# DFT over 3136 points factored 56 by 56 instead of 64 by 49, step 1 in products of 256 columns, and six forms of the block of step 2 and residual

## The chip, the cores and the metric

The kernel runs on one core of one Trainium2 chip (trn2). The metric is the device time of one execution in microseconds (us); lower is better.

## The reference

What must be computed, cut to what matters (batch 8, sequence 3136, width 256; 4*256 = 1024 hidden):

```
def _attn_ref(x):
    X = np.fft.fft(x, axis=1)          # over 3136 positions
    X = np.fft.fft(X, axis=2)          # over 256 channels
    return X.real.astype(np.float32)

def _moe_ref(x, g_ln, w_ch1, w_ch2):
    mu, var = mean and variance of x over the channels
    xn = (x - mu) / np.sqrt(var + 1e-06) * g_ln
    ch = np.maximum(xn @ w_ch1, 0.0) @ w_ch2
    return (x + ch).astype(np.float32)
```

The input of the second function is the output of the first.

## The kernel before

The transform over 3136 positions is split as 64 times 49. **Step 1** (`step1`, L247) multiplies by the 64-point table, for two positions of the 49 at a time (both parities stacked on 128 partitions). The positions are paired by symmetry, so there are 14 slots of pairs, taken two at a time in 7 units per batch. For batch 0 the products are in full f32 (L255, L257); for batches 1 to 7 each operand is split in a rounded f32r part and its rest, and the unit is three f32r products of 512 columns with stationary tables of 128 by 128 (L262: `fl` with `t1_hi`, `fh` with `t1_lo`, `fh` with `t1_hi`). The folds that make the operands are `fold_zw` and `fold_eo` (L207 to L214) and `fold_lo` (L225), on POOL from batch 1 on. The result is copied to `s1` by ACT (L265), stored to DRAM (`store1`, L269), and read back with positions on partitions (`relayout`, L276). `ends` and `step1_ends` (L184, L233) do the same for two leftover channels with small f32 products (L237, L238, L241).

**Step 2** (`step2`, L299) multiplies by the twiddled 49-point tables in full f32: 16 groups of two units per batch, 98 columns each (99 and an extra product with 50 columns, L313, for the group that holds frequency 0), two products a group. One call does two groups, so there are 8 calls a batch and 64 in all. Each f32 product appears in the trace as two weight loads and two matmul instructions. ACT and DVE take the result from PSUM into the chunk `ck` and its f32r parts `ckh`, `ckl` (L330 to L334).

The rest works on **chunks** of 256 frequencies (49 of them, the last one 264 wide), in **slots** `s = 8c + f` for chunk `c` and hidden block `f`. In each slot `moe1_a` (L354) does 6 f32r products of 256 columns and `moe2` (L404) does 12, the latter for the hidden block three slots earlier; between them ACT and DVE make the hidden values (L359 to L369). `residual` (L422, products at L428) does the channel transform of the chunk in full f32 with 129 and 130 columns, for two halves `i` of the chunk; it gives the residual and the norm's statistics. `finish` (L473) joins both.

The order of each engine is written out by hand. The main loop runs over the slots; what else is done in a slot stands in two lists, `late` (before `moe2`) and `after` (behind it). `step2` for chunk `c + 1` and `residual` for chunk `c` are both put behind slot `8c + 5`, in that order; this run of f32 products is called the **block** below. `steps1` places the 7 units of step 1 of a batch at slots counted back from the slot `need`, at which the batch is first used; `behind` shifts a unit by two slots where a block has two calls of `step2`. Most units stand at the slot of a block and so directly behind it, since `joined` is added last. PSUM has one bank with the tag `y`, which serves step 1 from batch 1 on, the ends, and every second `step2` of a block with two.

Before the loop, the start loads `x` of batch 0 and the weights, runs step 1 of batch 0 on PE as the units arrive, stores, reads back, and converts the weights (given as 64-bit words) on DVE and ACT.

The loop of slots reads:

```
for s in range(6, last):
    moe1_b(s - 1)
    moe1_a(s)
    for fn, args in late.get(s, ()):
        fn(*args)
    moe2(s - lag)
    for fn, args in after.get(s, ()):
        fn(*args)
```

Of the kernel before, what the change touches and what calls it, by code (L numbers as in the profile page):

```python
# [51 lines left out]
def runs():

    units = [unit for g in range(16) for unit in (g, 16 + g)]
    return [r for unit in units for r in (((49, unit),) if unit else ((24, 64), (24, 32)))]


def group_bounds():
    return [0] + [99 + 98 * g for g in range(16)]


def tables():
    u = np.arange(64)[:, None]
    t1 = np.zeros((64, 64))
    t1[:, :33] = np.cos(2 * np.pi * u * np.arange(33) / 64)
    t1[:, 33:] = np.sin(2 * np.pi * u * np.arange(1, 32) / 64)
    th = np.zeros((64, 64))
    th[:, 1:32] = -np.sin(2 * np.pi * u * np.arange(1, 32) / 64)
    th[:, 33:] = np.cos(2 * np.pi * u * np.arange(1, 32) / 64)
    tu = np.zeros((128, 388))  # L70
    for par in range(2):
        s = slice(64 * par, 64 * par + 64)
        tu[s, s] = t1
        tu[s, 128 + 64 * par:192 + 64 * par] = -t1
        tu[s, 256 + 64 * par:320 + 64 * par] = th
        tu[s, 384 + 2 * par] = 1.0
        tu[s, 385 + 2 * par] = np.cos(np.pi * np.arange(64))
    vs = ((0, np.arange(1, 15)), (1, np.append(np.arange(15, NV), 0)))
# [68 lines left out]
def tile_kernel(ctx: ExitStack, tc: tile.TileContext, x, g_ln, w1, w2, tu, tab, tz, ty, tw, out):  # L147
# [710 lines left out]
```

## Time and profile before

| | |
|---|---|
| median of 2 runs | 1009.55 us (1008.93 to 1010.18) |
| span of the profiled execution | 1008.9 us |
| granted clock of TensorE, mean | 1.000 of full speed |
| busy: PE / PE weight loads / DVE / ACT / POOL | 99% / 97% / 81% / 53% / 25% |
| matmul instructions | 8289 |

The profiled execution agrees with the lower of the two runs. "PE" is the matmul row, "PEld" the weight loads beside it. The ends of matmuls are modelled, so successive matmuls overlap in the listing and a busy share says little; the distance from one start to the next is what PE really spends on one. A group of rows in the profile gives the mean of the listed durations, in ns.

### The profile page before, as it was taken

What the parts mean: (1) busy time and instruction counts of PE and PEld (TensorE: products, weight loads), DVE (VectorE), ACT (ScalarE), POOL (GpSimd) and SP (SyncE); (2) the same over time, 40 slices, a digit from 0 to 9 for tenths busy, and PEclk for the clock granted to TensorE, in tenths of its full rate; (3) what the DMA queues carried; (4) which work ended last, traced back from release to release, by engine and by line L of the source; (5) the groups of instructions that cost most, each with busy time, mean ns of one, the idle gap of its engine ahead of it and who ended that gap; (6) DMA issues with size and microseconds to landing.
All of it is one profiled execution on the core that took longest, in us unless ns stands there. A gap on an engine that the chain in (4) does not pass through costs nothing.

```text
span 1008.9 us, 21765 instructions
## 1 busy us (share of the span) xinstructions
PE 998.4 (99%) x8289; PEld 976.5 (97%) x8289; DVE 817.2 (81%) x2190; ACT 534.7 (53%) x1416; POOL 248.5 (25%) x278
## 2 busy tenths in 40 slices
PE   9899999999999999999999999999999999999998
PEld 6699999999999999999999999999999999999998
DVE  6688887888778788878887888888788878887887
ACT  3555555555555555555555555554555554554553
POOL 1146533134213232312341224123323200000000
PEclk9999999999999999999999999999999999999999
DMA  9943352214221261121521242211311112100101
GB/s 343 265 164 95 116 168 74 85 53 136 85 93 55 74 177 65 56 85 60 158 84 54 84 130 91 94 54 63 116 43 43 54 55 83 41 24 22 43 22 43
DMA packets 41528, 92.10 MB, mean 91 GB/s; under 512 B 4176, under 2 KB 18704, under 8 KB 40528
## 3 DMA queue, kind: packets, MB, share of 16 engines
q1 hardware_dynamic: 40016, 88.87, 26.8%
q8 instruction: 66, 1.08, 0.5%
q0 software_dynamic: 320, 1.05, 0.3%
q10 hardware_dynamic: 1088, 0.79, 0.2%
q14 instruction: 38, 0.31, 0.1%
HBM read 50.32 MB, written 40.37 MB: 90 GB/s over the span
## 4 chain that ended last, share of the span: by engine, by line
PE 93%; DVE 4%; ACT 2%; DMA 1%; issue 0%; SPq 0%; DVEq 0%; ACTq 0%
PE acc L404 51%; PE ab L354 26%; PE ps L309 6%; PE psy L428 4%; PE ps L262 3%; DVE h_lo L369 1%; PE pw L682 1%; PE ps L255 1%; DMA scratch<-s 1%; PE ps L257 1%; DVE h L360 1%; DVE h L361 1%; ACT h_hi L368 0%; DMA s<-scratch 0%; ACT asb L359 0%
## 5 line engine op out<-in xcount | busy, mean ns | idle before, releaser
L404 PE MATMUL acc<-w_hi,h_lo 128*128 128x256 f32 x1568 | 437.9, 279 | 0.2 <-DVE h_lo L369 0.2
L404 PE MATMUL acc<-w_lo,h_hi 128*128 128x256 f32 x1568 | 437.7, 279 | 0.0
L404 PE MATMUL acc<-w_hi,h_hi 128*128 128x256 f32 x1568 | 437.6, 279 | 0.0
L368 ACT ACTIVATE h_hi<-h 128x512 fp32r<-128x512 f32 x392 | 249.3, 636 | 308.4 <-DVE h L361 308.3
L369 DVE SCALAR_TENSOR_TENSOR h_lo<-h,h_hi 128x512 fp32r<-128x512 f32 x392 | 282.0, 719 | 158.1 <-ACT h_hi L368 157.0
L404 PEld LDWEIGHTS acc<-w_hi,h_lo 128*128 128x128 f32 x1568 | 296.7, 189 | 0.6 <-DVE h_lo L369 0.4
L404 PEld LDWEIGHTS acc<-w_lo,h_hi 128*128 128x128 f32 x1568 | 295.4, 188 | 0.0
L404 PEld LDWEIGHTS acc<-w_hi,h_hi 128*128 128x128 f32 x1568 | 295.1, 188 | 0.0
L354 PE MATMUL ab<-ckl,w_hi 128*128 128x256 f32 x768 | 218.5, 285 | 1.8 <-DVE h L361 1.8
L354 PE MATMUL ab<-ckh,w_lo 128*128 128x256 f32 x768 | 214.9, 280 | 0.5 <-ACT ckh L330 0.3
L354 PE MATMUL ab<-ckh,w_hi 128*128 128x256 f32 x768 | 214.5, 279 | 0.0
L225 POOL TENSOR_TENSOR fl<-f,fh 128x512 fp32r<-128x512 f32 x49 | 64.2, 1309 | 518.6 <-ACT fh L219 512.4
L360 DVE TENSOR_TENSOR h<-asb,ab 128x256 f32<-128x256 f32 x384 | 158.2, 412 | 1.5 <-ACT asb L359 1.5
L361 DVE TENSOR_TENSOR h<-asb,ab 128x256 f32<-128x256 f32 x384 | 158.1, 412 | 0.0
L354 PEld LDWEIGHTS ab<-ckl,w_hi 128*128 128x128 f32 x768 | 145.3, 189 | 5.9 <-ACT w_hi L539 1.5
L354 PEld LDWEIGHTS ab<-ckh,w_lo 128*128 128x128 f32 x768 | 144.7, 188 | 3.1 <-ACT ckh L330 0.5
L354 PEld LDWEIGHTS ab<-ckh,w_hi 128*128 128x128 f32 x768 | 144.6, 188 | 0.0
L359 ACT COPY asb<-ab 128x256 f32<-128x256 f32 x384 | 137.8, 359 | 8.1 <-PE ab L354 6.2
L265 ACT COPY s<-ps 128x508 f32<-128x508 f32 x56 | 32.7, 584 | 64.9 <-PE ps L262 51.0
L309 PE MATMUL ps<-tab_s,s 112*128 112x98 f32 (+1 forms) x512 | 65.6, 273 | 1.5 <-DMA s<-scratch 1.5
L309 PEld LDWEIGHTS ps<-tab_s,s 112*128 112x128 f32 x512 | 61.9, 192 | 2.0 <-issue 2.0
L330 ACT CAST ckh<-ps 128x392 fp32r<-128x392 f32 (+49 forms) x112 | 39.7, 356 | 40.6 <-PE ps L309 40.4
(108 smaller groups left out, 980.5 us busy)
## 6 DMA issues: line engine op xcount, KB each, us to landing
xs<-x SPq DMA_DIRECT2D x56, 512.0 KB, 3.8
out<-o SPq DMA_DIRECT2D x96, 256.0 KB, 2.0
scratch<-s SPq DMA_DIRECT2D x49, 256.0 KB, 2.3
s<-scratch SPq DMA_DIRECT2D x7, 1792.0 KB, 9.8
w1p_all<-w SPq DMA_DIRECT2D x8, 512.0 KB, 8.3
scratch<-s POOLq DMA_DIRECT2D x4, 256.0 KB, 6.3
s<-scratch SPq DMA_DIRECT2D x2, 448.0 KB, 5.3
s<-scratch SPq DMA_DIRECT2D x1, 896.0 KB, 11.2
```

What stands on the lines that cost most here:

```text
L225: nc.gpsimd.tensor_tensor(out=lo, in0=f, in1=hi.bitcast(F32), op=ALU.subtract)
L265: nc.scalar.copy(s[:, :, :, :127], ps[:, :, :, :127])
L309: nc.tensor.matmul(ps[:, h, k0 - base:k1 - base], s2[b][:KP, g, 128 * h:128 * h + 128], tab_s[:, h, k0:k1], start=(h == 0 and g == 2 * j), ...
L330: nc.scalar.copy(hi, src)
L354: nc.tensor.matmul(pt, wt[wi][:, j, fs], ch[xi][:, j, :w], start=(n == 0), stop=(n == 2))
L359: nc.scalar.copy(asb[:, :w], pa)
L360: nc.vector.tensor_tensor(out=h[:, :w], in0=asb[:, :w], in1=pb, op=ALU.add)
L361: nc.vector.tensor_tensor(out=h[:, w:], in0=asb[:, :m], in1=pb[:, :m], op=ALU.subtract)
L368: nc.scalar.activation(h_hi, h, AF.Relu)
L369: nc.vector.scalar_tensor_tensor(out=h_lo, in0=h, scalar=0.0, in1=h_hi.bitcast(F32), op0=ALU.max, op1=ALU.subtract)
L404: nc.tensor.matmul(acc[c, i][:, side], hs[xi][:, h0:h0 + 128], ws[wi][:, f], start=(f == 0 and side == 0 and n == 0), stop=(f == 7 and n = ...
L428: nc.tensor.matmul(ps[:, j, :129 + j], ck[:, j], ty_s[:, j, :129 + j], start=(j == 0), stop=True, skip_group_check=True)
```

## The change

The DFT is factored 56 by 56. A unit has 56 frequencies; there are 14 groups a batch, 112 columns each, 7 calls of `step2` a batch and 56 in all. The slots of pairs are now 15: 7 units of two slots, and an eighth unit (index `NU`) of one slot, which holds the positions that are multiples of 56 and has its own input `x0` and its own tile `xz`. Step 1 works on 112 partitions with tables of 112 by 112. From batch 1 on, step 1 does its three passes for each slot by itself, in products of 256 columns: six products for a unit of two slots, three for the eighth. Units of step 1 stand at fixed distances before `need`, and none of them at the slot of a block.

Each chunk has one of six forms of the block: 0 as before; 1, 2 and 5 give the first product of a half 130 columns instead of 129 (half 0, both halves, half 1); 4 swaps the two products of half 1; 3 puts the residual ahead of `step2`. The table `tw_all` moves from a buffer of its own into one of the three buffers of `ckh`.

```
-NS = 14
+R1 = 56
+XP = 2 * R1
+NU = 7
+NS = 2 * NU + 1
+NG = 14
...
-    tw_all = const.tile([128, 640], F32, name="tw_all")
+    tw_all = moving.tile([128, 2, CKW], F32R, tag="ck_hi", name="tw_all", bufs=3).bitcast(F32)
...
     def load_x(b, i):
-        in_order(nc.sync.dma_start(xs[:, i], x[b, i]))
+        if i == NU:
+            in_order(nc.sync.dma_start(xz[:R1], x0[b]))
+        else:
+            in_order(nc.sync.dma_start(xs[:, i], x[b, i]))
...
+    def slots(i):
+        return 1 if i == NU else 2
+
+    def fold_eo(b, i, eng=nc.gpsimd):
+        n = slots(i)
+        z, w = zw.pop((b, i)) if n > 1 else (xz[:, None, 1:129], xz[:, None, 255:127:-1])
...
+        if b == 0 and n == 1:
+            nc.tensor.matmul(ps, tu_p, pieces.pop((b, i))[0], start=True, stop=True)
+        elif b == 0:
...
             p = pieces.pop((b, i))
-            for n, (ti, xi) in enumerate(PASSES):
-                nc.tensor.matmul(ps, (t1_hi, t1_lo)[ti], p[xi],
-                                 start=(n == 0), stop=(n == 2))
+            for a in range(n):
+                for j, (ti, xi) in enumerate(PASSES):
+                    nc.tensor.matmul(ps[:, a], (t1_hi, t1_lo)[ti], p[xi][:, a],
+                                     start=(a == 0 and j == 0), stop=(j == 2),
+                                     skip_group_check=True)
...
+    forms = [(c % 6 + c // 6) % 6 for c in range(LC)] + [0]
...
-        for j in range(2):
-            nc.tensor.matmul(ps[:, j, :129 + j], ck[:, j], ty_s[:, j, :129 + j],
-                             start=(j == 0), stop=True, skip_group_check=True)
+        form = forms[c]
+        wide = {1: (0,), 2: (0, 1), 5: (1,)}.get(form, ())
+        order = (1, 0) if form == 4 and i == 1 else (0, 1)
+        for j in order:
+            n = 130 if j or i in wide else 129
+            nc.tensor.matmul(ps[:, j, :n], ck[:, j], ty_s[:, j, :n],
+                             start=(j == order[0]), stop=True, skip_group_check=True)
...
+    for c in range(LC):
+        if forms[c] == 3:
+            for i in range(2):
+                add(8 * c + (5 if c > 1 else 6), residual, c, i)
...
-    steps1 = {1: [17, 20, 23, 26, 28, 31, 34]}
-    for b in range(2, NB):
-        need = 8 * (b * REG // CW) - 3
-        steps1[b] = sorted([need - 46, need - 45] +
-                           [behind(need - d) for d in (56, 40, 32, 24, 16)])
     for b in range(1, NB):
         need = 8 * (b * REG // CW) - 3
+        behind = (54, 45, 38, 30, 25, 21, 14, 34)
+        at = [need - d for d in behind] if b > 1 else [17, 20, 23, 28, 30, 33, 35, 25]
+        ends_at = need - (55 if b > 1 else 30)
...
             fold_zw(0, 3, nc.vector)
+            fold_eo(0, NU)
             step1(0, 3)
+            step1(0, NU)
```

On PE, in the kernel before, a block of chunk 19 reads as follows; `ps2` is step 2, `psy` the residual, `ps1` step 1 of batch 4, `ab` and `acc` the products of the main loop.

```order
L404 MATMUL acc19_1_6339<-w2_hi_73,h_hi154_6313 128x256
L309 MATMUL ps2_27_6407<-tab_s_81,s2_3_5345 128x98 x4
L428 MATMUL psy19_0_6419<-ty_s_85,ck19_5802 128x129
L428 MATMUL psy19_0_6419<-ty_s_85,ck19_5802 128x130
L428 MATMUL psy19_1_6422<-ty_s_85,ck19_5802 128x129
L428 MATMUL psy19_1_6422<-ty_s_85,ck19_5802 128x130
L262 MATMUL ps1_4_4_6425<-fl4_4_6311,t1_hi_78 128x512
L262 MATMUL ps1_4_4_6425<-fh4_4_6276,t1_lo_79 128x512
L262 MATMUL ps1_4_4_6425<-fh4_4_6276,t1_hi_78 128x512
L354 MATMUL ab158_6435<-ckl19_5804,w1_hi_76 128x256
```

In the changed kernel the block of chunk 15, which has form 5, stands between main products alone on PE.

```order
L433 MATMUL acc15_1_5191<-w2_hi_73,h_hi122_5165 128x256
L338 MATMUL ps2_19_5263<-tab_s_81,s2_2_3570 128x112 x4
L462 MATMUL psy15_0_5275<-ty_s_85,ck15_4654 128x129
L462 MATMUL psy15_0_5275<-ty_s_85,ck15_4654 128x130
L462 MATMUL psy15_1_5278<-ty_s_85,ck15_4654 128x130 x2
L383 MATMUL ab126_5285<-ckl15_4656,w1_hi_76 128x256
```

No step 1 follows a block any more; the main products do, and the second half of this one has 130 columns twice.

A unit of step 1 in the changed kernel (batch 2, unit 1), on PE:

```order
L290 MATMUL ps1_2_1_2291<-fl2_1_2172,t1_hi_78 112x256
L290 MATMUL ps1_2_1_2291<-fh2_1_2120,t1_lo_79 112x256
L290 MATMUL ps1_2_1_2291<-fh2_1_2120,t1_hi_78 112x256
L290 MATMUL ps1_2_1_2291<-fl2_1_2172,t1_hi_78 112x256
L290 MATMUL ps1_2_1_2291<-fh2_1_2120,t1_lo_79 112x256
L290 MATMUL ps1_2_1_2291<-fh2_1_2120,t1_hi_78 112x256
```

Three products of 512 columns have become six of 256, somewhere between the main products of two slots.

At the start, PE of the changed kernel has one product more, `ps1_0_7` of the eighth unit, between units 3 and 4 of batch 0:

```order
L285 MATMUL ps1_0_3_189<-zw0_3_183,tu_s_80 112x2x128
L279 MATMUL ps1_0_7_195<-f0_7_186,tu_s_80 112x256
L284 MATMUL ps1_0_4_203<-zw0_4_200,tu_s_80 112x2x128
L285 MATMUL ps1_0_4_203<-zw0_4_200,tu_s_80 112x2x128
L284 MATMUL ps1_0_4_203<-zw0_4_200,tu_s_80 112x2x128
```

Its operand `f0_7` is made on POOL, behind the two stores of step 1 and an addition for the ends (`e0c0`) that stood there before too:

```order
L298 DMA scratch0_138<-s1_0_137 112x2x256 [waits Activation_49]
L298 DMA scratch0_138<-s1_0_137 112x2x256
L208 TENSOR_TENSOR e0c0_132<-xs_87 112x8 [waits DMAHW7_49,DMAHW0_49]
L239 TENSOR_TENSOR f0_7_186<-xz_88 112x128 [waits DMAHW4_49,Pool_49]
L240 TENSOR_TENSOR f0_7_186<-xz_88 112x128
```

The two folds and the product that reads them are new; the rows around them keep their order.

## Rows read from the trace of the kernel before

**Rows 1.** The profile's page: busy time of each engine, and the chain of work that ended last by engine, in shares of the span.

```profile
PE 998.4 (99%) x8289; PEld 976.5 (97%) x8289; DVE 817.2 (81%) x2190; ACT 534.7 (53%) x1416; POOL 248.5 (25%) x278
PE 93%; DVE 4%; ACT 2%; DMA 1%; issue 0%; SPq 0%; DVEq 0%; ACTq 0%
```

**Rows 2.** The view of waits, PE alone: the two longest in total (who waited for whom: us in total, times, longest).

```profile
PE ab L354 <- DVE h L361: 1.8, 5, 0.8
PE ps L309 <- DMA s<-scratch: 1.5, 1, 1.5
```

**Rows 3.** Groups of instructions of PE by line and shape, whole span (out<-in, shapes, count | busy us, mean ns of one | idle before).

```profile
L404 PE MATMUL acc<-w_hi,h_hi 128*128 128x256 f32 x1568 | 437.6, 279 | 0.0
L354 PE MATMUL ab<-ckh,w_hi 128*128 128x256 f32 x768 | 214.5, 279 | 0.0
L309 PE MATMUL ps<-tab_s,s 112*128 112x98 f32 x480 | 61.0, 273 | 0.0
...
L262 PE MATMUL ps<-fl,t_hi 128*128 128x512 f32 x49 | 21.1, 430 | 1.2 <-DVE ckl L334 1.2
...
L309 PE MATMUL ps<-tab_s,s 112*128 112x99 f32 x32 | 4.8, 271 | 1.5 <-DMA s<-scratch 1.5
```

**Rows 4.** The timeline of PE: the first product of a stretch of 144 main products, the block that ends it, and the first product of step 1 behind that block (start us, us, then the instruction).

```profile
313.18 0.28 PE L354 MATMUL ab<-ckl,w_hi 128*128 128x256 f32 x1
...
330.14 1.03 PE L309 MATMUL ps<-tab_s,s 112*128 112x98 f32 x8
...
331.84 0.48 PE L262 MATMUL ps<-fl,t_hi 128*128 128x512 f32 x1
```

**Rows 5.** The timeline of PE around another block, the first and the seventh of the 144 main products behind it, and the block that ends them.

```profile
843.97 1.03 PE L309 MATMUL ps<-tab_s,s 112*128 112x98 f32 x8
844.83 1.08 PE L428 MATMUL psy<-ty_s,ck 128*128 128x129 f32 x8
845.67 0.36 PE L354 MATMUL ab<-ckl,w_hi 128*128 128x256 f32 x1
...
846.46 0.28 PE L404 MATMUL acc<-w_hi,h_lo 128*128 128x256 f32 x1
...
862.10 0.69 PE L309 MATMUL ps<-tab_s,s 112*128 112x98 f32 x5
```

**Rows 6.** Groups of PE by shape in two windows: one row of 313.2 to 330.1 us (the stretch of rows 4), and one of 845.75 to 862.05 us (the stretch of rows 5).

```profile
L404 PE MATMUL acc<-w_hi,h_hi 128*128 128x256 f32 x32 | 9.0, 281 | 0.0
...
L404 PE MATMUL acc<-w_hi,h_hi 128*128 128x256 f32 x32 | 8.8, 276 | 0.0
```

**Rows 7.** The timeline of PE at one unit of step 1 (its first product, and the main product behind its third), and then groups of PE by shape in three windows, one row of each: 510.1 to 514.2 us (between a block and that unit), 514.95 to 517.05 us (between it and the next unit), 517.8 to 527.9 us (behind the next unit).

```profile
514.25 0.39 PE L262 MATMUL ps<-fl,t_hi 128*128 128x512 f32 x1
...
514.94 0.28 PE L354 MATMUL ab<-ckl,w_hi 128*128 128x256 f32 x1
...
L404 PE MATMUL acc<-w_hi,h_hi 128*128 128x256 f32 x8 | 2.2, 276 | 0.0
...
L404 PE MATMUL acc<-w_hi,h_lo 128*128 128x256 f32 x4 | 1.1, 281 | 0.0
...
L404 PE MATMUL acc<-w_hi,h_hi 128*128 128x256 f32 x20 | 5.5, 276 | 0.0
```

**Rows 8.** Groups of PE by shape in five windows, one row of each, the windows lying directly behind these: the block at 211.7 us (214.4 to 218.5), the block at 974.7 us (976.5 to 980.7), the block at 547.4 us (550.1 to 554.1), the block at 956.6 us (958.4 to 974.7), the ends at 246.8 us (247.5 to 251.4).

```profile
L404 PE MATMUL acc<-w_hi,h_hi 128*128 128x256 f32 x7 | 2.0, 281 | 0.0
...
L404 PE MATMUL acc<-w_lo,h_hi 128*128 128x256 f32 x8 | 2.2, 281 | 0.0
...
L404 PE MATMUL acc<-w_lo,h_hi 128*128 128x256 f32 x8 | 2.2, 276 | 0.0
...
L404 PE MATMUL acc<-w_lo,h_hi 128*128 128x256 f32 x32 | 8.8, 276 | 0.0
...
L404 PE MATMUL acc<-w_hi,h_hi 128*128 128x256 f32 x7 | 1.9, 276 | 0.0
```

**Rows 9.** The timeline of PE's weight loads at the ends of a batch: two loads of 128 columns, two of 112 columns, and the next.

```profile
365.49 0.30 PEld L238 LDWEIGHTS pse<-e0c,tu_s 128*128 128x128 f32 x2
365.71 0.28 PEld L241 LDWEIGHTS pse<-one,masked 128*112 128x112 f32 x2
365.91 0.19 PEld L354 LDWEIGHTS ab<-ckl,w_hi 128*128 128x128 f32 x1
```

**Rows 10.** The timeline of PE at a block with two calls of step 2.

```profile
468.15 1.93 PE L309 MATMUL ps<-tab_s,s 112*128 112x98 f32 x16
469.91 1.08 PE L428 MATMUL psy<-ty_s,ck 128*128 128x129 f32 x8
```

**Rows 11.** The timeline of PE at the start: the last products of unit 3 of batch 0, the first of unit 4, and the first product of step 2.

```profile
15.04 0.60 PE L257 MATMUL ps<-zw,tu_s 128*128 128x256 f32 x2
15.47 0.38 PE L255 MATMUL ps<-zw,tu_s 128*128 128x256 f32 x1
...
34.28 0.66 PE L309 MATMUL ps<-tab_s,s 112*128 112x99 f32 x4 [1.54 <-DMA s<-scratch]
```

**Rows 12.** POOL: the timeline at the same place, and the two groups of its folds, whole span.

```profile
14.46 1.62 POOL L269 DMA_DIRECT2D scratch<-s  x2 [3.94 <-ACT s L243]
16.11 0.23 POOL L190 TENSOR_TENSOR e0c<-xs 128x8 f32<-128x8 f32 x1
...
L214 POOL TENSOR_TENSOR f<-zw 128x256 f32<-128x256 f32 x49 | 50.2, 1024 | 0.0
L213 POOL TENSOR_TENSOR f<-zw 128x256 f32<-128x256 f32 x49 | 39.2, 799 | 3.1
```

**Rows 13.** The timeline of DVE ahead of the block at 862.10 us: the last read of the bank that the residual's second half takes next.

```profile
861.30 0.47 DVE L479 SCALAR_TENSOR_TENSOR o<-acc,r,y 128x256 f32<-128x256 f32 x1
```

More of the change, by code (lines that the diff above doesn't have):

```diff
@@ L39 @@
 HW = 576
-NS = 14
+R1 = 56
[3 more added lines that the diff above has]
+NG = 14
+KP = 8 * 2 * NU + 4
+KZ = 4 * NS
+NM = NG // 2
 ROWS = NB * N
-NU = NS // 2
-KP = 8 * NS
 def unit_k(unit):
     if unit == 0:
-        return np.concatenate([[0, N // 2], 64 * np.arange(1, 25), 32 + 64 * np.arange(24)])
-    return unit + 64 * np.arange(49)
+        return np.concatenate([[0, N // 2], R1 * np.arange(1, 28), 28 + R1 * np.arange(28)])
+    return unit + R1 * np.arange(R1)
 def runs():
-    units = [unit for g in range(16) for unit in (g, 16 + g)]
-    return [r for unit in units for r in (((49, unit),) if unit else ((24, 64), (24, 32)))]
+    units = [unit for g in range(NG) for unit in (g, NG + g)]
+    return [r for unit in units for r in (((R1, unit),) if unit else ((27, R1), (28, 28)))]
@@ L58, in group_bounds @@
 def group_bounds():
-    return [0] + [99 + 98 * g for g in range(16)]
-def tables():
[L63 to L70, printed above, removed]
-    for par in range(2):
[L72 to L78, printed above, removed]
+    return [0] + [2 * R1 + 1 + 2 * R1 * g for g in range(NG)]
@@ L240, in step1_ends @@
         if p1 == NS:
-            nc.tensor.matmul(ps[:KP, 2, 0:1], masked, one, start=False, stop=True,
+            nc.tensor.matmul(ps[:KZ, 2, 0:1], masked, one[:XP], start=False, stop=True,
                              skip_group_check=True)
-        nc.scalar.copy(s1[b][:, p0:p1, :, 127], ps[:, 0:2].rearrange("p h s -> p s h"))
+        nc.scalar.copy(s1[b][:, p0:p1, :, 127], ps[:XP, 0:2].rearrange("p h s -> p s h"))
         if p1 == NS:
-            nc.scalar.copy(zmu[:, b % 2, 127:128], ps[:KP, 2, 0:1])
+            nc.scalar.copy(zmu[:, b % 2, 127:128], ps[:KZ, 2, 0:1])
@@ L247, in step1 @@
     def step1(b, i):
         alloc1(b)
+        n = slots(i)
         ps = psum.tile([128, 2, 2, 128], F32, tag="y" if b else f"acc{i % 2}", name=f"ps1_{b}_{i}",
-                       bufs=1 if b else 2)
-        if b == 0:
+                       bufs=1 if b else 2)[:XP, :n]
+        if b == 0 and n == 1:
+            nc.tensor.matmul(ps, tu_p, pieces.pop((b, i))[0], start=True, stop=True)
+        elif b == 0:
             z, w = zw.pop((b, i))
-            for h in range(2):
+            for h, t in ((0, tu_p), (1, tu_n)):
@@ L312, in step2 @@
             if g == 0:
-                nc.tensor.matmul(ps[:, 1, 0:50], zmu[:, b % 2], tz_s, start=False, stop=True,
+                nc.tensor.matmul(ps[:, 1, 0:R1 + 1], zmu[:, b % 2], tz_s, start=False, stop=True,
                                  skip_group_check=True)
@@ L616, in tile_kernel @@
     first = {}
-    for m in range(3, 64):
+    for m in range(3, NM * NB):
         s = 8 * (first_token(m) // CW) - 3
@@ L658, in tile_kernel @@
         for i in range(2):
-            add(s, residual, c, i)
+            if forms[c] != 3:
+                add(s, residual, c, i)
             add_late(s + 1, residual_e, c, i)
@@ L665, in tile_kernel @@
         add(d, step1, b, i)
-        add(d, store1, b, i)
+        if i < NU:
+            add(d, store1, b, i)
     add_late(8 * LC - 2, singles)
@@ L765, in tile_kernel @@
             nc.sync.dma_start(tab_s[:, :, gb[8]:], tab[:, :, gb[8]:])
-            for i in range(NU):
+            for i in range(NU + 1):
                 load_x(1, i)
```

159 lines of the change are left out of this document (89 added, 70 removed).

## The prediction

> **What bounds the kernel now.** I read the page first. PE is busy 99% of the span and makes up 93% of the chain that ended last [rows 1]; what it waits for is 1.8 us on DVE and 1.5 us on the first read-back, the two longest entries of the view of waits [rows 2]. So the time is what PE spends from one product to the next, and the other engines matter at the start and where they would come late. The groups by shape give the counts: three passes of 1568 in `moe2` and of 768 in `moe1_a` make 7008 main products of 256 columns [rows 3].
>
> Their pace is what I looked at next, and it is not one number. In the stretch from 313.18 to 330.14 us there are 144 products: 16.96 / 144 = 117.8 ns each [rows 4]. In the stretch behind the block at 843.97 us the products from the seventh on take (862.10 - 846.46) / 138 = 113.3 ns [rows 5]. No wait stands between them in either. The listed duration tells which pace holds: 281 ns in the first, 276 ns in the second [rows 6]. Over the whole kernel the mean is 437.6 us / 1568 = 279.1 ns [rows 3], so a share of (281 - 279.1) / 5 = 0.38 of the main products ran at the fast pace. If all did, PE would save 0.62 x 7008 x 4.5 ns = 19.5 us; if none did, it would lose 12 us. This lottery is larger than every other term here.
>
> What sets the pace? A stretch keeps it until PE does something else. Behind a block it is fast or slow: slow at 211.7 and 974.7 us, fast at 547.4 and 956.6 us [rows 8]. These four are the first and the last of each kind that holds steadily. I went through all blocks that have no step 1 directly behind them: 13 of 26 lead to the fast pace. The 7 with the extra product for frequency 0 all do (the one at 508 us leads to the fast window at 510.1 us [rows 7]); of the other 19 only 6 do. Three products of 512 columns turn the fast pace to slow and then slow to fast: 276 ns before a unit of step 1, 281 behind it, 276 behind the next [rows 7]. And where step 1 follows a block directly, as at 331.84 us [rows 4], all 18 stretches behind are slow. The ends of a batch lead to the fast pace in 5 of 7 cases, one of them at 247.5 us [rows 8].
>
> **The change part by part.** Let a be the share of products at the fast pace after the change.
>
> Main products and step 1. Before, the main products cost 7008 x (117.8 - 0.38 x 4.5) = 813.6 us. Step 1 has 49 units of 0.69 us (514.25 to 514.94 [rows 7]), 33.8 us. After, there are 15 slots x 3 passes x 7 batches = 315 products of 256 columns instead of 147 of 512. No row shows an f32r product of 256 columns with a table of 112 columns; I bound it by the two paces, 113.3 and 117.8 ns, and count it with the main products. That makes 7323 x (117.8 - 4.5a) = 862.6 - 33.0a. The difference is 15.2 - 33.0a us.
>
> Weight loads of 112 columns. In the ends two loads of 128 columns start 0.22 us before the next, two of 112 columns 0.20 us [rows 9], so one is about 10 ns shorter. The Trainium skill, "TensorE: Matmul & The Clock Gate", section "LDWEIGHTS (loading the stationary operand)", makes the load proportional to the columns; the trace agrees in the sense of it. I take no gain for it, since the main products' loads stay at 128 columns, but it is why the six products might act on the pace of what follows.
>
> Step 2. Before: 512 matmul instructions of 98 or 99 columns [rows 3]. After: 14 groups x 2 x 2 x 8 = 448 of 112 or 113. Sixteen of them span 468.15 to 469.91 us, 110 ns each [rows 10], and eight of the residual with 129 and 130 columns span 0.84 us, 105 ns [rows 5]. Since 98 columns do not go faster than 130, 112 columns cost what 98 do: 64 x 110 ns = 7.0 us saved. The bounds are 0 (if the time went with the columns, whose sum does not change) and 7.0; I take 7.0, because a wider shape at the same spacing stands in the rows. The columns added by forms 1, 2 and 5 cost nothing by the same rows.
>
> The start. PE goes from unit 3 to unit 4 of batch 0 at 15.47 us without a wait [rows 11]. The new product between them needs the two folds on POOL, which stand behind two stores and the addition that ends at 16.34 us [rows 12]. Folds of 256 columns take 799 and 1024 ns [rows 12]; half of it is 0.9 us. So the product can start at about 17.25 us, 1.8 us late, and takes 0.43 us itself (a pair of 256-column f32 products, 15.04 to 15.47 [rows 11]): +2.2 us. It is on the path, since the store of the last unit, the read-back and the first step 2 at 34.28 us follow, and PE stands waiting for the read-back there [rows 11]. Bounds: 0 if the smaller loads of `x` make up for it, 3 us if the longer last store (three slots instead of two) adds to it. I take 2.2.
>
> The rest. POOL gets two smaller folds and two copies more per batch, at 25% busy; ACT and DVE copy as much as before in fewer pieces, at 53% and 81% [rows 1]. PE is what covers them, and none of them comes last in a wait of more than 1.8 us [rows 2]. SP issues one more load per batch, of 56 rows. `tw_all` in a buffer of `ckh` delays nobody: its last reader is done at the start, and the third chunk is far behind. Form 3 moves step 2 behind the residual, so its result is 0.84 us later (844.83 to 845.67 [rows 5]); `ck` is needed only three slots on, some 6 us. Its residual needs the bank that DVE reads until 861.77 us [rows 13], 0.33 us before the block [rows 5], and only for the second half; so no wait.
>
> Sum: 15.2 - 33.0a - 7.0 + 2.2 = 10.4 - 33.0a us. With a = 0.38 as before it is -2.1; it breaks even at a = 0.315; a = 1 gives -22.6 and a = 0 gives +10.4.
>
> **The value of a.** Of 48 stretches 7 are opened by the block with frequency 0 (fast in 7 of 7), 7 are reset by the ends one slot behind the block (5 of 7), and 34 by other blocks. Of these, blocks entered at the fast pace led to slow in 7 of 8, blocks entered at the slow pace led to fast in 5 of 11; alternating, this is fast in about 0.3 of cases. That holds for form 0, one in six. For the five other forms no row exists, and I take one half: 0.47 in all. Together (7 + 5 + 16) / 48 = 0.58. The units of step 1 no longer stand at a block, where they brought 18 slow stretches; whether six products of 256 columns flip the pace is open, and pulls towards one half. I take 0.55: -7.75 us. From the span of 1008.9 us that is 1001.15; the median of the runs is 0.65 us above that span, so 1001.8 us.
>
> By the rule of the Trainium skill, "TensorE: Matmul & The Clock Gate", section "Back-to-back issue gap" (columns at 2.4 GHz plus 2.5 ns: 109 ns for 256, 216 for 512), there would be no two paces; by it step 1 would cost 2.7 us more and no pace would be won, so the sum would be -2.1 us, the time of rival 1. The trace contradicts it with 113.3 and 117.8 ns.
>
> **The rivals.** (1) The pace stays as it was, a = 0.32 to 0.42: the forms change nothing and only the units' new places count. For it: nothing ties a form to a pace in any row. Against it: the 18 slow stretches had step 1 directly behind the block. Time: -2.1 us, 1007.5. (2) Nearly all fast, a above 0.75: the six products with shorter loads bring PE back to the fast pace each time, and most chunks hold one or two units. For it: the loads' 10 ns. Against it: products of 512 columns, whose loads have far more room, also turn fast to slow [rows 7]. At a = 0.9: -19.3 us, 990. (3) The other side: slower than before. Products of step 1 turn the pace to slow in the chunks that hold them, or blocks alternate as form 0 does; it decides from a below 0.315. At a = 0.1: +7.1 us, 1016.7. Against it: the blocks with frequency 0 and the ends alone give a = 0.25. (4) Form 3 does not hide: 8 chunks x 0.84 us = 6.7 us, on top of the forecast 1008.5.
>
> **How the numbers follow.** Forecast (a from 0.42 to 0.75, 995 to 1006): 0.45. Rival 1: 0.14. Rival 2: 0.25. Rival 3: 0.13. Rival 4: 0.03. A run of this kernel tells about 2% from no change, that is below 989.4 or above 1029.7 us. Below 989.4 needs a over 0.93, about half of rival 2: 0.13. Above 1029.7 nothing here reaches but a wait added to rival 3: 0.02. Same: 0.85. The range runs from a = 0.97 (987.5) to a = 0.15 with a little on top (1015).
>
> **What would show it right or wrong.** The mean of the `moe2` groups should be 278.2 ns (a = 0.55) against 279.1; 276 would be rival 2, 280.5 rival 3. Step 2 should count 448 instructions at 110 ns spacing. The first step 2 should start near 36.5 us. Behind a unit of step 1 the mean should show whether it flips the pace. I am wrong if PE gets waits in the loop, or if the pace has other values than these two.

## The result: 5.5 us slower, with most main products at the fast pace

Before 1009.55 us, after 1015.03 us; ratio 1.0053, interval 1.0035 to 1.007. The forecast was 1001.8 us. Two large terms stand behind this, of opposite sign. One execution of the run e2, told of below, ran at a granted clock of 0.557 and took 1649.06 us; the time given for e2 is that of its other three.

The page of after, its busy times and its chain, to set beside [rows 1]: PE is busy for 7 us less, yet the chain that ended last is PE only for 83%, with 8% on DMA.

```profile
PE 991.2 (98%) x8394; PEld 972.4 (96%) x8395; DVE 814.2 (80%) x2182; ACT 537.2 (53%) x1415; POOL 260.8 (26%) x309
...
PE 83%; DMA 8%; DVE 5%; ACT 1%; issue 1%; POOL 1%; SPq 0%; POOLq 0%; DVEq 0%; ACTq 0%
```

Groups of PE by line and shape, after. L433 is `moe2`, L383 `moe1_a`, L338 step 2, L290 step 1, L342 the product for frequency 0 [rows 3].

```profile
L433 PE MATMUL acc<-w_hi,h_hi 128*128 128x256 f32 x1568 | 433.9, 277 | 0.0
...
L383 PE MATMUL ab<-ckh,w_hi 128*128 128x256 f32 x768 | 213.4, 278 | 0.0
L338 PE MATMUL ps<-tab_s,s 116*128 116x112 f32 x416 | 56.7, 282 | 0.0
...
L290 PE MATMUL ps<-fl,t_hi 112*112 112x256 f32 x105 | 29.8, 284 | 0.0
...
L338 PE MATMUL ps<-tab_s,s 116*128 116x113 f32 x32 | 5.4, 296 | 9.3 <-DMA s<-scratch 9.3
...
L342 PE MATMUL ps<-tz_s,zmu 60*128 60x57 f32 x16 | 3.7, 311 | 0.0
```

The gain: `moe2` went from 279 to 277 ns, nearly the fast pace of 276, and a unit of step 1 that PE reaches at the fast pace mostly leaves it so. Around the unit at 255.40 us, 251.5 to 255.3 and 256.2 to 268.3 us, one row of each (compare [rows 7]):

```profile
L433 PE MATMUL acc<-w_hi,h_hi 128*128 128x256 f32 x8 | 2.2, 276 | 0.0
...
L433 PE MATMUL acc<-w_hi,h_hi 128*128 128x256 f32 x24 | 6.6, 276 | 0.0
```

The loss: PE waits twice for the read-back, 9.3 us in all where it was 1.5 [rows 2]. The view of waits of after, and then the timeline of PE at the first step 2 of batch 0, the first main product, and the first step 2 of batch 1 [rows 11]:

```profile
PE ps L338 <- DMA s<-scratch: 9.3, 2, 5.8
PE ps L279 <- POOL f L240: 2.1, 1, 2.1
```

```profile
42.16 1.17 PE L338 MATMUL ps<-tab_s,s 116*128 116x113 f32 x4 [5.81 <-DMA s<-scratch]
43.26 0.67 PE L342 MATMUL ps<-tz_s,zmu 60*128 60x57 f32 x2
43.86 2.90 PE L338 MATMUL ps<-tab_s,s 116*128 116x112 f32 x12
47.06 0.58 PE L383 MATMUL ab<-ckh,w_lo 128*128 128x256 f32 x1 [0.30 <-ACT ckh L359]
...
169.65 0.70 PE L338 MATMUL ps<-tab_s,s 116*128 116x113 f32 x4 [3.49 <-DMA s<-scratch]
```

Why the read-back is late shows in the windows. A row has the window and its length, then the busy time and the count of PE, PEld, DVE, ACT and POOL; the last three numbers are the granted clock, the share of the 16 DMA engines, and GB/s. In the first, in which PE stands still, loads of 116 rows are nearly all that moves: 94 GB/s on a quarter of the engines. The second lies mostly behind the wait: the clock is at 0.50, the lower of the two levels, 1.2 GHz, and the twelve matmul instructions of step 2 take 2.90 us (1.59 us in e1, at full clock). The third and the fourth show how long the clock stayed there, and a second such stretch, which begins right behind a wait of 1.55 us for DVE that ends at 88.85 us. A third goes from 171.1 to 174.5 us, behind the second wait for the read-back.

```profile
39.50:41.50 2.00, 0.00 (x0) 0.00 (x0) 0.00 (x0) 0.00 (x0) 0.00 (x0) 0.97 0.25 94
...
41.60:47.00 5.40, 4.60 (x18) 4.06 (x18) 0.62 (x1) 0.74 (x2) 0.00 (x0) 0.50 0.28 102
...
41.40:51.60 10.20, 9.14 (x37) 8.40 (x38) 3.36 (x8) 2.94 (x8) 1.28 (x1) 0.50 0.46 141
89.20:92.50 3.30, 3.30 (x18) 3.30 (x17) 2.60 (x5) 2.02 (x10) 3.22 (x4) 0.50 0.27 97
```

The same transfer of before, right after its issue for batch 1 and with stores of `out` beside it, fills all of them:

```profile
130.50:134.50 4.00, 4.00 (x37) 4.00 (x36) 3.41 (x8) 2.47 (x9) 1.10 (x2) 1.00 1.05 295
```

The transfer takes its rows from the sum of step 2, 112 before and 116 after. The Trainium skill, "DMA: Bandwidth & Descriptors", section "Why a DMA increments its semaphore by 16 and not by 1", says that a DMA takes the largest number of engines, up to 16, that divides the slowest dimension of both of its patterns. An estimate from that rule is 4 engines for 116 rows and 15 for 120. The traces agree: a share of 0.25 with 116 rows, and 0.93 with 120 in e1 below.

Time of PE from each product's start to the next's, summed by kind over the span (us; worked out from the trace, waits counted with the product ahead of them; what lies behind the last main product, 3.8 us, is left out). e3 and f5 are runs told of below.

| | before | after | e3 | f5 |
|---|---|---|---|---|
| 7008 main products | 823.2 | 815.6 | 808.6 | 806.9 |
| step 1, batches 1 to 7 | 36.1 | 38.1 | 38.1 | 33.7 |
| step 2 | 56.7 | 53.4 | 51.5 | 56.6 |
| frequency 0 | 1.5 | 3.1 | 2.8 | 1.5 |
| residual | 41.7 | 44.0 | 43.2 | 42.0 |
| start, ends, weights | 44.5 | 54.4 | 47.2 | 44.8 |
| time of the runs | 1009.55 | 1015.03 | 998.45 | 992.04 |

By stages: the first main product starts at 47.06 instead of 36.85 us (+10.2); from there to the first main product behind the first step 2 of batch 1 (174.53 against 154.92 us) it takes 127.5 instead of 118.1 us (+9.4); from there on after is 14.6 us faster. In e1 the same three are 40.61 us, 119.1 us and, from there on, the time of after: the number of rows alone accounts for 6.4 of the 10.2 us and for 8.4 of the 9.4.

### The profile page after: what moved, and what is told of

It reads as the page before. It is cut to its first block, busy times and chain, and to the rows that moved or that the text cites. A ratio compares the mean times of both kernels' runs of the same rounds, so it can differ in the third digit from the quotient of the medians.

```text
span 1013.8 us, 22039 instructions
## 1 busy us (share of the span) xinstructions
PE 991.2 (98%) x8394; PEld 972.4 (96%) x8395; DVE 814.2 (80%) x2182; ACT 537.2 (53%) x1415; POOL 260.8 (26%) x309
## 4 chain that ended last, share of the span: by engine, by line
PE 83%; DMA 8%; DVE 5%; ACT 1%; issue 1%; POOL 1%; SPq 0%; POOLq 0%; DVEq 0%; ACTq 0%
PE acc L433 46%; PE ab L383 24%; PE ps L338 5%; PE psy L462 4%; PE ps L290 3%; DMA s<-scratch 3%; DMA xs<-x 3%; DMA ty_s<-ty 2%; DVE h_lo L398 2%; DMA scratch<-s 1%; ACT h_hi L397 1%; DVE h L389 1%; DVE h L390 1%; PE ps L342 0%; DVE st L484 0%
## 5 line engine op out<-in xcount | busy, mean ns | idle before, releaser
L433 PE MATMUL acc<-w_hi,h_lo 128*128 128x256 f32 x1568 | 434.0, 277 | 0.4 <-DVE o L525 0.3
L433 PE MATMUL acc<-w_lo,h_hi 128*128 128x256 f32 x1568 | 433.9, 277 | 0.0
L433 PE MATMUL acc<-w_hi,h_hi 128*128 128x256 f32 x1568 | 433.9, 277 | 0.0
L398 DVE SCALAR_TENSOR_TENSOR h_lo<-h,h_hi 128x512 fp32r<-128x512 f32 x392 | 288.5, 736 | 154.4 <-ACT h_hi L397 148.9
L433 PEld LDWEIGHTS acc<-w_hi,h_lo 128*128 128x128 f32 x1568 | 295.1, 188 | 0.8 <-DVE o L525 0.5
L433 PEld LDWEIGHTS acc<-w_lo,h_hi 128*128 128x128 f32 x1568 | 295.0, 188 | 0.2 <-POOL w_lo L574 0.2
L433 PEld LDWEIGHTS acc<-w_hi,h_hi 128*128 128x128 f32 x1568 | 295.1, 188 | 0.0
L383 PE MATMUL ab<-ckl,w_hi 128*128 128x256 f32 x768 | 219.9, 286 | 2.4 <-DVE ckl L363 1.5
L383 PE MATMUL ab<-ckh,w_lo 128*128 128x256 f32 x768 | 214.1, 279 | 0.8 <-ACT w_lo L625 0.5
L383 PE MATMUL ab<-ckh,w_hi 128*128 128x256 f32 x768 | 213.4, 278 | 0.0
L251 POOL TENSOR_TENSOR fl<-f,fh 112x512 fp32r<-112x512 f32 (+1 forms) x56 | 69.3, 1238 | 493.4 <-ACT fh L245 493.4
L383 PEld LDWEIGHTS ab<-ckl,w_hi 128*128 128x128 f32 x768 | 145.4, 189 | 3.2 <-issue 1.9
L383 PEld LDWEIGHTS ab<-ckh,w_lo 128*128 128x128 f32 x768 | 145.5, 189 | 1.4 <-ACT w_lo L625 0.7
L383 PEld LDWEIGHTS ab<-ckh,w_hi 128*128 128x128 f32 x768 | 145.3, 189 | 0.0
L293 ACT COPY s<-ps 112x508 f32<-112x508 f32 (+1 forms) x64 | 35.7, 557 | 74.1 <-PE ps L290 57.1
L338 PE MATMUL ps<-tab_s,s 116*128 116x112 f32 (+1 forms) x448 | 62.2, 283 | 9.3 <-DMA s<-scratch 9.3
L359 ACT CAST ckh<-ps 128x448 fp32r<-128x448 f32 (+49 forms) x104 | 38.3, 371 | 59.7 <-PE ps L338 59.7
L338 PEld LDWEIGHTS ps<-tab_s,s 116*128 116x128 f32 x448 | 57.0, 199 | 10.5 <-issue 6.3
```

Of the source, the lines that this page charges most:

```text
L251: nc.gpsimd.tensor_tensor(out=lo, in0=f, in1=hi.bitcast(F32), op=ALU.subtract)
L293: nc.scalar.copy(s1[b][:, 2 * i:2 * i + n, :, :127], ps[:, :, :, :127])
L338: nc.tensor.matmul(ps[:, h, k0 - base:k1 - base], s2[b][:KP, g, 128 * h:128 * h + 128], tab_s[:, h, k0:k1], start=(h == 0 and g == 2 * j), ...
L359: nc.scalar.copy(hi, src)
L383: nc.tensor.matmul(pt, wt[wi][:, j, fs], ch[xi][:, j, :w], start=(n == 0), stop=(n == 2))
L398: nc.vector.scalar_tensor_tensor(out=h_lo, in0=h, scalar=0.0, in1=h_hi.bitcast(F32), op0=ALU.max, op1=ALU.subtract)
```

## Experiments

Times are medians of the runs, ratios are to the kernel before, run beside each. "Fast" and "slow" below are the two paces, 113.3 and 117.8 ns. A block "F to F" was entered at the fast pace and left for it, by the mean step of the last 18 main products of the stretches on both sides; stretches that are too short to tell or have a wait in them are left out.

**The read-back (e1 to e3).** e1: after, with 120 rows read back, step 2 still using 116.

```
+KR = 120
-        in_order(eng.dma_start(s2[b][:KP, g0:g1]..., sv[:KP, ...
+        in_order(eng.dma_start(s2[b][:KR, g0:g1]..., sv[:KR, ...
```

> The changed kernel, with the read-back of a batch's step 1 taking 120 rows in one DMA instead of 116 (4 rows more, not used). Theory D: a DMA of 116 rows runs on a quarter of the 16 DMA engines (in the changed kernel the read-backs show a busy share of 0.25 and about 100 GB/s, before, with 112 rows, 250 to 340 GB/s). Then the first read-back lands in about 5 us instead of 9.2, the read-back of batch 1 in under 10 us instead of 21.8, PE's waits for read-backs fall from 9.3 us to about 2, and the time to 1003 to 1007 us. Rival: the start is lost to contention and to the late fold, not to the number of rows; then 1013 to 1016 us and the waits for read-backs stay above 8 us.

1000.63 us, ratio 0.991 (0.9893 to 0.9926): 14.4 us less than after, more than either theory expected. The waits for read-backs fell by 7.6 us (9.3 to 1.7); the rest goes with the stretches at the lower clock, 17 us in after, of which e1 has none (granted clock 1.000 over the span, 0.992 in after). Timeline of e1 at the first step 2, and the window right after the read-back of batch 1 was issued, now at 0.93 of the engines:

```profile
37.76 0.67 PE L339 MATMUL ps<-tab_s,s 116*128 116x113 f32 x4 [1.69 <-DMA s<-scratch]
```

```profile
138.80:142.80 4.00, 4.00 (x38) 3.96 (x36) 2.42 (x6) 3.23 (x13) 0.00 (x0) 1.00 0.93 201
```

e2 gives step 2's table 120 rows too (`tab_s = const.tile([KR, 2, HALF], ...)`). e3 adds the fold of the 8th unit ahead of the first ends on POOL (`fold_eo(0, NU)` before `ends(0, 0, 6)`).

> As the run before, with the table of step 2 loaded in 120 rows as well (its last 4 rows are not used). Theory D: the three loads of the table (1.4 MB in all) also go from a quarter of the engines to all, what queues behind them at the start (the table of the channel transform, x of batch 1) comes earlier, and the time falls by another 2 to 8 us, to 997 to 1004 us. Rival: the table loads are hidden behind the first chunks; then the same as the run before within 1 us.

> As the run before, with the fold of the eighth unit of batch 0 issued on POOL ahead of its first addition, so that it does not stand behind two stores. In the changed kernel PE waits 2.05 us for it. Theory: the wait is on the path of the start; the time falls by 2 to 3.6 us, to 994 to 1001 us. Rival: the read-back that follows is bound by something else; then within 1 us of the run before.

e2 999.27 us (ratio 0.9902, 0.9886 to 0.9919; 998.25 to 1001.41), e3 998.45 us (0.989, 0.9875 to 0.9905). Both together are worth 2.2 us against e1. How much of it is the table's and how much the fold's is not settled, since the three times of e2 lie further apart than that. The traces of e1 and e3 put 1.2 us of it ahead of the first main product (39.43 instead of 40.61 us), where the wait for the fold is gone but one of 1.0 us for an addition of the ends on POOL has come in its place, and 1.0 us behind it.

**What sets the pace: forms, size, place (e4 to e8, f1).** e4 is e3 with form 0 in all chunks; e8 the kernel before with the six forms; e5 is e3 with step 1 in products of 512 columns; e6 the kernel before with 256; e7 the kernel before with all units two slots behind the blocks; f1 is e6 and e7 together.

```
e4: -    forms = [(c % 6 + c // 6) % 6 for c in range(LC)] + [0]
    +    forms = [0] * NCH
e6: -            nc.tensor.matmul(ps, (t1_hi, t1_lo)[ti], p[xi], ...
    +            nc.tensor.matmul(ps[:, a], (t1_hi, t1_lo)[ti], p[xi][:, a], ...   (for a in range(2))
e7: -        return s + 2 * (len(first[s]) > 1)
    +        return s + 2
```

> As the run before, with form 0 for all chunks. Theory P (the place and size of step 1 give the fast pace): the mean of the moe2 groups stays at 277 ns and the time within 2 us of the run before. Theory F (the six forms give it): the mean goes back to 278.5 to 279.5 ns and the time rises by 10 to 18 us.

> The kernel before, with the six forms of the block by turns and nothing else. Theory F (the forms give the fast pace): mean of the moe2 groups near 277 ns, 992 to 1000 us. Theories S and P: where step 1 stands at a block it sets the pace, so the mean stays at 278.5 to 279.5 ns and the time within 5 us of 1009.5.

> The changed kernel with the read-back and the table of step 2 in 120 rows and the early fold, and with step 1 of batches 1 to 7 in products of 512 columns again, at the places of the changed kernel and with its tables of 112 columns. Theory S (the size of the products decides): each unit of three turns the pace, as in the kernel before; the mean of the moe2 groups rises from 277 to 278.5 ns or more and the time by 8 to 18 us over the same kernel with 256 columns. Theory P (the place decides, away from the blocks): the mean stays at 277 ns, the time within 2 us of it.

> The kernel before, with step 1 of batches 1 to 7 in six products of 256 columns a unit, at its old places. Theory S: the stretches behind a block and its unit become fast, the mean of the moe2 groups falls from 279.1 to 277 ns and the time by 10 to 18 us, to 992 to 1000 us. Theory P: the units at the blocks still lead to the slow pace; the mean stays at 278.5 to 279.5 ns and the time within 4 us of 1009.5.

> The kernel before, with every unit of step 1 that stood at a block moved two slots behind it, still in products of 512 columns. Theory P: the pace becomes fast in most stretches, mean about 277 ns, 992 to 1000 us. Theory S: the pace still turns at each unit, mean 278.5 to 279.5 ns, within 6 us of 1009.5.

> The kernel before (64 by 49) with both edits that were tried apart: every unit of step 1 two slots behind the block, and its products of 256 columns (six per unit). Two readings of the traces differ here. Theory A (size and place of step 1's products are all there is): the gains add up, the main products fall to the 115.4 ns of the kernel with the fold moved ahead, 14.6 us less than before: about 995 us. Theory B (step 2's own products of 98 columns are a second thing that turns the pace): with units of 512 columns off the blocks, 33 of the blocks led from the fast pace to the slow one and 37 units led back; units of 256 columns keep whatever pace they find (F to F and S to S). Then the blocks leave the slow pace and nothing brings the fast one back: moe2 mean near 279 to 280 ns, 1003 to 1010 us.

| run | us | ratio (interval) | blocks F to F / F to S | units F to F / F to S / S to F / S to S |
|---|---|---|---|---|
| e3 | 998.45 | 0.989 (0.9875 to 0.9905) | 38 / 1 | 35 / 3 / 5 / 0 |
| e4 | 998.57 | 0.9894 (0.988 to 0.9909) | 39 / 0 | 37 / 3 / 3 / 0 |
| e8 | 1007.5 | 0.9972 (0.9961 to 0.9983) | 8 / 5 | 1 / 15 / 9 / 1 |
| e5 | 1013.87 | 1.0038 (1.0028 to 1.0048) | 11 / 1 | 0 / 26 / 7 / 14 |
| e6 | 1008.5 | 0.9985 (0.9976 to 0.9995) | 4 / 9 | 16 / 1 / 0 / 11 |
| e7 | 1001.57 | 0.9911 (0.9892 to 0.993) | 5 / 34 | 0 / 9 / 37 / 0 |
| f1 | 1006.43 | 0.9963 (0.995 to 0.9976) | 8 / 16 | 24 / 1 / 0 / 21 |

Blocks with step 1 right behind them (before, e6, e8) are not in these counts; the 7 cases S to F of e5 are its units of one slot, which have products of 256 columns. The forms do next to nothing: e4 equals e3, and e8 is 0.3% below its kernel before. What a unit does depends on its columns and on the layout. With tables of 128 by 128, units of 512 columns turn the pace either way (e7), and units of 256 keep what they find (e6, f1). With tables of 112 by 112, units of 512 columns lead to the slow pace from either (e5: 26 times from fast, 14 from slow), and units of 256 keep the fast pace and bring it back from the slow one (e3: 35 of 38 and 5 of 5; the one-slot units of e5: 7 of 7). Groups of e5 ahead of the unit at 200.54 us and behind it, one row of each of the windows 197 to 200.5 and 201.4 to 211.8 us:

```profile
L431 PE MATMUL acc<-w_hi,h_hi 128*128 128x256 f32 x8 | 2.2, 276 | 0.0
...
L431 PE MATMUL acc<-w_hi,h_hi 128*128 128x256 f32 x20 | 5.6, 281 | 0.0
```

Units of 256 columns that PE reaches at the slow pace, a row ahead of the unit and one behind it each: first 56 by 56 (f6, told of below, the unit at 339.85 us, windows 336 to 339.8 and 340.7 to 351), then 64 by 49 (f1, the unit at 296.41 us, windows 293 to 296.3 and 297.2 to 309.6):

```profile
L435 PE MATMUL acc<-w_hi,h_hi 128*128 128x256 f32 x8 | 2.2, 281 | 0.0
...
L435 PE MATMUL acc<-w_hi,h_hi 128*128 128x256 f32 x20 | 5.5, 276 | 0.0
```

```profile
L406 PE MATMUL acc<-w_hi,h_hi 128*128 128x256 f32 x8 | 2.2, 281 | 0.0
...
L406 PE MATMUL acc<-w_hi,h_hi 128*128 128x256 f32 x23 | 6.5, 281 | 0.0
```

In 56 by 56 the size is worth 15.4 us (e5 against e3). In 64 by 49 it is not: there the blocks themselves turn the pace (f1: 16 of 24 from fast to slow, 16 of 23 from slow to fast), in e7 the next unit of 512 columns brings the fast one back (37 times), and units of 256 columns leave the slow one (f1). e7 falls between what its two theories expected. So size and place do not add up, and something else makes the blocks of 56 by 56 keep the pace.

**What lets a block keep the pace (f2 to f4).** f2 is f1 with step 2's products widened to 112 columns, some of them taken twice; f3 is e3 with 112 of step 2's 116 rows, the last four left out of the sums; f4 is f1 with four rows of zeros added to step 2's 112.

```
f2: +    nc.tensor.matmul(ps[:, h, k0 - base:k0 - base + 112], ..., tab_s[:, h, q:q + 112], ...
f3: +    nc.tensor.matmul(..., s2[b][:112, ...], tab_s[:112, h, k0:k1], ...
f4: +    nc.tensor.matmul(..., s2[b][:116, ...], tab_s[:116, h, k0:k1], ...
```

> The kernel of the run before it, with step 2's products widened from 98 to 112 columns, the columns taken twice so that the sums in them are not the reference's. Theory B (the width of step 2's products): blocks lead to the fast pace as they do in 56 by 56, moe2 mean 276 to 277 ns; main products 12 to 14 us less than in the 98-column kernel if that one is slow; step 2 adds some 1 to 3 us; about 996 to 999 us. Theory A, or a theory by which the rows of the tables (112 instead of 128 in step 1 and its ends) make the pace: the mean of moe2 is that of the 98-column kernel within 0.7 ns, the time within 3 us of it.

> The kernel with the fold moved ahead (56 by 56, 998.45 us), step 2's products taking 112 of their 116 rows; the last four rows are left out of the sums. Nothing else is changed: columns, places, loads and the read-back are the same. Theory R (the 116 rows of step 2's products are what lets a block lead to the fast pace): blocks become a lottery as they are in 64 by 49, units of 256 columns keep what they find, moe2 mean 278 to 279.5 ns instead of 276.5, some 7 to 13 us more: 1005 to 1011 us. Rival U (the tables of 112 rows in step 1 and the ends, or the banks' layout, make the pace): no change, 997 to 1000 us.

> The kernel before (64 by 49) with units off the blocks and products of 256 columns (1006.43 us), and four rows of zeros added to both operands of step 2, so that its products take 116 rows; the step-2 table is loaded in 128 rows, the read-back stays at 112, POOL clears rows 96 to 127 of the buffer ahead of each read-back (DVE in the first batch). Theory R: blocks lead to the fast pace, moe2 mean 276 to 277 ns, main products 10 to 14 us less: 993 to 997 us, which would be below every kernel so far. Rival U: moe2 mean 278 to 279 ns as without the rows, 1004 to 1009 us.

f2 1005.41 us (0.9954, 0.9938 to 0.997), f3 998.9 us (0.9891, 0.9875 to 0.9907), f4 1006.62 us (0.9964, 0.9953 to 0.9976). Neither the columns nor the rows of step 2 do it: theories B and R both fell.

**An address (f5 to f7, g1 to g3).** A difference not yet tried is where the constants lie. The smaller `tu_s` and the move of `tw_all` into a buffer of `ckh` shift what follows, and the residual's table `ty_s` goes from byte 148576 to 145856 of its partition: from 32 bytes over a multiple of 64 onto one. The edit is a dummy tile:

```
+    const.tile([128, 8], F32, name="pad")
     minus = const.tile([128, 128], F32R, name="minus")
     ty_s = const.tile([128, 2, 130], F32, name="ty_s")
```

f5 is f1 with it, f6 is e3 with it (`ty_s` goes off the multiple), f7 the kernel before with it alone. In g1, which is f1, the pad stands behind `ty_s`. In g2, also f1, it stands ahead of step 2's table `tab_s`, so that `tab_s` comes onto a multiple of 64 as well. g3, which is e3, has two pads, ahead of `tab_s` and ahead of `minus`: `tab_s` comes onto a multiple of 64, and `ty_s` moves by 64 bytes and stays on one.

> The kernel before (64 by 49) with units of step 1 off the blocks and products of 256 columns (1006.43 us), and a 32-byte pad ahead of the constants minus, ty_s, xs and zmu, which puts the residual's table ty_s on a multiple of 64 bytes, where it lies in 56 by 56. Theory D (the address of the residual's table): blocks lead to the fast pace, moe2 mean 276 to 277 ns, 993 to 997 us. Rival: the address does nothing, moe2 mean 278 to 279 ns, 1004 to 1009 us.

> The 56 by 56 kernel with the fold moved ahead (998.45 us) and the same 32-byte pad, which puts ty_s 32 bytes over a multiple of 64, where it lies in the kernel before. Theory D: blocks become a lottery, moe2 mean 278 to 279.5 ns, 1004 to 1011 us. Rival: no change, 997 to 1000 us.

> The kernel before with the 32-byte pad alone. Theory D: blocks lead to the fast pace, units of 512 columns still turn it, those at the blocks too: between 998 and 1006 us. Rival: 1008 to 1011 us.

> The 64 by 49 kernel with units off the blocks and products of 256 columns, the 32-byte pad put behind ty_s: xs, zmu and all that follows move to multiples of 64 as in the run of 992.04 us, ty_s and minus stay 32 bytes over one. Theory D (it is the residual's table): no gain, 1004 to 1009 us, moe2 mean 278 to 279 ns. Rival (xs, zmu or a buffer behind them): 991 to 994 us, 276 ns.

> The same kernel with the pad ahead of step 2's table tab_s, so that tab_s as well as ty_s, minus, xs and zmu lie on multiples of 64 bytes (tz_s then lies 32 over one). If only ty_s counts: 991 to 994 us, as with the pad behind tab_s. If step 2's table has a part of its own: step 2 loses up to 0.1 us at each of its 56 blocks, 987 to 990 us.

> The 56 by 56 kernel with the fold moved ahead (998.45 us), tab_s moved to a multiple of 64 bytes and ty_s kept on one. If only ty_s counts: 997 to 1000 us. If step 2's table has a part of its own: 993 to 996 us.

| run | `ty_s` over a multiple of 64 | us | ratio (interval) | blocks F to F / F to S |
|---|---|---|---|---|
| f1 | 32 | 1006.43 | 0.9963 (0.995 to 0.9976) | 8 / 16 |
| g1 | 32 | 1006.61 | 0.9969 (0.9956 to 0.9982) | 6 / 16 |
| f5 | 0 | 992.04 | 0.9823 (0.9809 to 0.9838) | 45 / 0 |
| g2 | 0, `tab_s` moved | 992.25 | 0.9827 (0.9812 to 0.9842) | 46 / 0 |
| f7 | 0 | 1000.83 | 0.9909 (0.9894 to 0.9924) | 21 / 1 |
| e3 | 0 | 998.45 | 0.989 (0.9875 to 0.9905) | 38 / 1 |
| f6 | 32 | 1003.88 | 0.9943 (0.9926 to 0.9959) | 17 / 18 |
| g3 | 0, 64 bytes further; `tab_s` moved | 1001.42 | 0.9925 (0.9908 to 0.9941) | 22 / 14 |

The same block in g1 and in f5, each a window ahead of it and one behind it (277.6 to 287.8 and 291.2 to 294.7 us in g1; 276.9 to 287 and 290.4 to 293.8 us in f5):

```profile
L407 PE MATMUL acc<-w_hi,h_hi 128*128 128x256 f32 x20 | 5.5, 276 | 0.0
...
L407 PE MATMUL acc<-w_hi,h_hi 128*128 128x256 f32 x8 | 2.2, 281 | 0.0
```

```profile
L407 PE MATMUL acc<-w_hi,h_hi 128*128 128x256 f32 x20 | 5.5, 276 | 0.0
...
L407 PE MATMUL acc<-w_hi,h_hi 128*128 128x256 f32 x8 | 2.2, 276 | 0.0
```

The two programs differ in 32 bytes in the place of `ty_s` and of `minus`, which the loop does not use. In 64 by 49 the address of the residual's table decides: 14.4 us between f1 and f5, 9 us in the kernel before alone. Only two places were tried there, bytes 148576 and 148608; that a multiple of 64 is what counts is a guess, not shown. In 56 by 56 it costs 5.4 us to move it off (f6), just under what was expected. The smaller loss fits what units do in the two layouts, though no run parts the two: blocks drop the pace in f6 too (18 of 35), but there units bring it back (16 of the 18 that were reached at the slow pace; 13 of 15 in g3), while in g1 none of 22 did. g3 loses 3 us although `ty_s` still lies on a multiple of 64, which no theory here expected; whether `tab_s` (and `tz_s`) does it, or the 64 bytes that `ty_s` and all behind it moved, was not tried. Why an operand of the block acts on the products behind it stays open.

f5 is faster than both kernels: 992.04 us, 17.8 us under its kernel before. Against e3 the table in the section on the result shows why 56 by 56 loses: step 2 saves 5.1 us, but step 1 costs 4.4, frequency 0 1.4, the start 2.4, the residual 1.2 and the main products 1.7 us more.

## Why the prediction was wrong, point by point

- **The bound and the two paces: right.** The same two values, 276 and 281 ns, hold the long stretches in the runs shown, and behind the start the time follows the share between them. The rule of the Trainium skill that the prediction sets against them ("TensorE: Matmul & The Clock Gate", section "Back-to-back issue gap") is given there for a product by itself; this stream, with a weight load for each product, does not test it.
- **The value of a: under-sized.** Of the 6662 steps of 112 to 120 ns between main products, 6126 are fast in after, a = 0.92 against 0.55 (before: 2575 of 6818, 0.38, as the prediction read it). The step that failed here is "For the five other forms ... I take one half": the forms are not what acts (e4, e8). Rival 2 came true in its mechanism: in after, the 7 units that were reached at the slow pace and can be told all led to the fast one. Its reason, the shorter loads, is not shown: with tables of 128 the same products keep the slow pace (21 of 21 in f1), but rows and columns of the table changed together. It is half of what acts; the other half, the place of `ty_s`, which keeps the blocks fast, was in no term. The prediction read of `tw_all` only that it "delays nobody"; that it moves the tables behind it was not asked.
- **Step 2: 7.0 us expected.** e3 saves 5.1 (56.7 to 51.5), where one figure of 110 ns was used for all. Most of the gap is at the product for frequency 0: in e3 the instruction of step 2 ahead of it takes 205 ns to the next start and the one behind it 200, eight times each (112 and 152 in before). The others lie near 112.
- **Step 1: inside its bounds in 64 by 49 only.** It was bounded by 113.3 and 117.8 ns a product; it took 121 ns with tables of 112 (38.1 / 315) and 114.7 with tables of 128 (f5). In before it took 36.1 us and not 33.8: the 0.69 us of one unit had been taken for all 49.
- **The start: the step that decided, and that failed.** It was put at +2.2 us with bounds of 0 to 3. The fold was right: PE waits 2.1 us for it, 1.8 was said. But "the store of the last unit, the read-back and the first step 2 at 34.28 us follow" took the read-back's duration from before, and "The rest" put the read-backs of the loop at nothing. The read-back went from all DMA engines to a quarter of them; the first main product came 10.2 us late and the loop lost another 9.4 us up to the first use of batch 1. Undoing the number of rows alone gives back 14.4 us (e1). What is left of the start in e1, +3.8 us, is still over the upper bound; in e3 it is +2.6.
- **The test that was named** ("I am wrong if PE gets waits in the loop") fired at 169.65 us. Rival 3 named the right side by the wrong mechanism: the pace was not lost but gained. With the read-back at full rate the kernel stands at 1000.63 us, near the forecast, from a larger gain of pace and a smaller saving elsewhere; that closeness is luck, a sum of errors.

## What to carry to other kernels

When a change alters the number of rows of a transfer, price the transfer again from the row count, before any compute term: 116 rows instead of 112 cost 14.4 us here, and step 2 gained 5.1 (e3). When a bound engine shows two paces, look at what decides between them by flipping one thing at a time, and include where the constants lie; removing a tile moves everything behind it. Count every direction, from slow to fast as well as from fast to slow, and do it in the layout in question: the same unit of 256 columns keeps the slow pace in one of these and ends it in the other. Effects on a pace do not add up: size, place and address gave 1.5, 8.5 and 9 us alone (e6, e7, f7), size and place together 3.3 (f1), all three 17.8 (f5).

## What the runs showed of the hardware that was not expected

- In 64 by 49, 32 bytes in the address of one moving operand (`ty_s`) decide whether the 256-column products behind its use stay at 113.3 ns each or go to 117.8 (g1 to f5: F to F in 6 of 22 blocks, then in 45 of 45).
- A short run of other products can set the pace of what follows, and which way differs with its columns and the layout: three products of 512 columns turn the pace either way with tables of 128 by 128 (e7: 37 of 37 from slow, 9 of 9 from fast) and lead to the slow one with tables of 112 by 112 (e5: 26 of 26 from fast, 14 of 14 from slow); six of 256 columns end the slow pace with tables of 112 (f6: 16 of 18) and keep it with tables of 128 (g1: 22 of 22).
- With the waits of 5.81 and 3.49 us the granted clock fell to 0.50: from 41.4 to 51.6 us, and from 171.1 to 174.5 us although PE had started again at 169.65. It fell once more from 89.2 to 92.5 us, where the wait ahead was 1.55 us. In e1, whose wait for the first read-back is 1.69 us, the clock is 1.000 over the span. A late transfer was paid for twice.
- Each of the two matmul instructions of the product for frequency 0 takes 178 ns from its start to the next with 60 rows and 57 columns (e3), and 91 ns with 112 rows and 50 columns (before); the instructions of step 2 on both sides are slower with it. Which of the two sizes does it was not tried.
